# Linear attention into a token-mixing feed-forward layer: U_high x and U_low x as rows of one operand, q's tail at full height, shorter norm statistics, subtractions on VectorE

## The chip, the cores and the metric

The kernel runs on one core of a Trainium2 chip. A core has TensorE (PE: matmuls, with a queue of weight loads of its own, PEld), VectorE (DVE), ScalarE (ACT), GpSimd (POOL) and SyncE (SP, which here issues all DMAs). They run side by side, each through its own instructions in order, and wait for each other by semaphores. The metric is device time in microseconds (us), the median of several runs.

## The reference

Eight batches of 576 tokens. Per batch, 8 heads of linear attention with an RMS norm, and then a layer that mixes tokens through a rank of 32 and applies a feed-forward block:

```python
kv = np.einsum('bhsd,bhse->bhde', k, v)              # 64 x 64 per head
out = np.einsum('bhsd,bhde->bhse', q, kv)            # 576 x 64 per head
rms = np.sqrt(np.mean(out * out, axis=-1, keepdims=True) + 1e-06)
x = (out / rms * g_norm)                             # heads side by side: (8, 576, 512)
h = x.transpose(0, 2, 1) @ U @ V                     # U: 576 x 32, V: 32 x 576
u = x + h.transpose(0, 2, 1)
ch = np.maximum(u @ w_ch1, 0.0) @ w_ch2              # 512 -> 2048 -> 512
return u + ch
```

U, V and the two matrices of the feed-forward block come as float64, everything else as float32.

## The kernel before

**Precision by parts.** TensorE multiplies float32 operands either in float32 or, faster, in a rounded form (`F32R`). For the second, an operand is split into a rounded high part and the low part that is left (`split`, `move` and `minus`), and a product is the sum of high x high, high x low and low x high. Weights arrive as float64 bit patterns and are decoded to float32 by a chain of bit operations (`decode`, five steps, four or five of them on VectorE), then split.

**Attention, per batch b and pair of heads p.** `kv_step` forms k^T v of two heads in one 128x128 block. `out_step` multiplies q by it: q lies transposed (128 rows of two heads, 576 token columns); the first 512 tokens are four float32 matmuls with 128 columns of q as weights (L235, into `big`), the last 64 tokens one with 64 columns (L237, into `small`). The profile records a float32 matmul of the program as two. ScalarE squares both. `stats_step` sums the squares on VectorE, takes the root on ScalarE and sharpens its reciprocal by one Newton step (seven steps on VectorE in all). `mul_step` writes x. `xsplit_step` splits x: `xh` on ScalarE (L102), `xl` for the first 512 tokens on GpSimd (L114), and the low part of the last 64 on VectorE (L278), put in the free lower half of the fifth block of `xh`. `turn_step` transposes x (VectorE and DMAs from batch 1 on, TensorE for batch 0). `t_step` multiplies by U: the weights are a U block of 64 columns, `u2` = [U_high, U_low], so that for batch 1 on the rows 0 to 31 of the result `tp` are U_high x and the rows 32 to 63 U_low x. For batch 0 other weights are used, `u4` = [U_high, U_high] and [U_low, U_low], in 14 matmuls instead of nine. `t4_step` makes of it a 128-row operand of high, high, low and low parts of the sum (for batch 1 on in six steps that go between ScalarE and VectorE), which `mix_step` multiplies by `v4`, V's parts in four matching blocks of rows, and adds to x; the result is scaled by g and split (`split_cols`).

**Feed-forward block.** Tokens go through in nine blocks j of 512. For each of 16 column blocks f of w_ch1, `ffn1` does 12 matmuls of 512 columns (L383 high x high, L384 high x low, L385 low x high); `relu` makes `hh` on ScalarE (L392) and `hl` on VectorE (L393); `ffn2` does 12 more (L400) one f later, when `hl` is there. `finish` adds u on VectorE (L411) and GpSimd (L412) and writes out.

**Order.** Attention of batch b+1 runs between the f of block b (`prep_schedule`). Batch 0 comes ahead of all by a table of positions (`PLAN`), and through block 0 the weights of each f are decoded and split two f ahead (L81 to L95; the low part on GpSimd). `ENG` names the engine of a step by a letter (a, v, g) for each pair. The order that this code gives is rearranged by the framework's own scheduler, with a modelled timeline; the program that comes out is fixed, engine by engine.

Of the kernel before, what the change touches and what calls it, by code (L numbers as in the profile page):

```python
# [47 lines left out]
def build(ctx: ExitStack, tc: tile.TileContext, kv_in, kvt0_in, kvt_in, q_in, uv_in, g_in, w_in, out):  # L48
# [180 lines left out]
    def out_step(b, p):  # L229
# [4 lines left out]
        for i in range(4):  # L234
            nc.tensor.matmul(big[:, i * P:(i + 1) * P], lhsT=qt[:, i * P:(i + 1) * P], rhs=kb, start=True, stop=True)  # L235
# [1 line left out]
        nc.tensor.matmul(small[0:TAIL, 0:P], lhsT=qt[:, MAIN:S], rhs=kb, start=True, stop=True)  # L237
# [4 lines left out]
    def stats_step(b, p):  # L242
        NS = 2 * NT
        ms = sm.tile([P, NS], F32, name="ms")
# [3 lines left out]
        nc.vector.tensor_reduce(out=ms.rearrange("p (i h) -> p i h", h=2), in_=xv, axis=AX.X, op=ALU.add)  # L248
# [3 lines left out]
        nc.vector.tensor_tensor(out=ta, in0=r0, in1=r0, op=ALU.mult)
        nc.vector.tensor_tensor(out=ta, in0=ta, in1=ms, op=ALU.mult)
# [42 lines left out]
    def t_step(b, p):  # L296
        xh, xl = state[b, p]["hl"]
        tp = bank()
        if b == 0:
            todo = [(u, xh, i) for u in u4 for i in range(NT)] + [(u4[0], xl, i) for i in range(4)]  # L300
            for n, (u, xx, i) in enumerate(todo):
                nc.tensor.matmul(tp[0:2 * R, 0:P], lhsT=u[:, i, :], rhs=xx[:, i, :], start=(n == 0), stop=(n == len(todo) - 1))
        else:
            for i in range(NT):
                nc.tensor.matmul(tp[0:2 * R, 0:P], lhsT=u2[:, i, :], rhs=xh[:, i, :], start=(i == 0), stop=(i == NT - 1))  # L305
                if i < 4:
                    nc.tensor.matmul(tp[0:2 * R, 0:P], lhsT=u2[:, i, :], rhs=xl[:, i, :], start=False, stop=False)
# [140 lines left out]
    u4t = weight_slot("u4", [P, 2, NT, 2 * R], F32R, 13)  # L448
    u4 = [u4t[:, n] for n in range(2)]
    for t in u4:  # L450
        nc.gpsimd.memset(t[:, 0, 0:1].bitcast(F32), 0.0)
# [181 lines left out]
```

## Time and profile before

| | |
|---|---|
| Median of three runs | 954.52 us (952.16 to 954.83) |
| Span of the profiled execution, first to last instruction | 949.2 us |
| Time of the profiled execution itself | not listed beside its span; the span is 5.3 us under the median of the runs |
| Mean granted clock of TensorE | 0.993 |
| Busy: PE, PEld, DVE, ACT, POOL | 923.2, 762.1, 439.6, 252.3, 135.4 us |
| Bytes moved by DMA | 65.49 MB |

Busy times are sums over the span; matmuls are pipelined, so their durations overlap and PE's busy time isn't PE at its peak. The start of one matmul to the start of the next is what it takes of TensorE. In rows by stage, a stretch is followed by its length, the busy time and the number of instructions of each engine, and at the end the granted clock, the DMA engines' share and GB/s. In rows of the timeline stand start, duration, engine, line, instruction, and in brackets the idle time ahead with what ended it. Groups of a line show the count, then the total busy us and the mean ns of one, then idle time and what ended it.

### The profile page before, as it was taken

How to read it: one execution, taken by the hardware profiler on the slowest of the kernel's cores; microseconds unless marked ns; L12 is line 12 of the kernel's file. 1: busy time of each engine (PE TensorE's matmuls, PEld its weight loads, DVE VectorE, ACT ScalarE, POOL GpSimd, SP SyncE). 2: the span in 40 equal slices, each digit the busy share in tenths (PEclk: the TensorE clock that was granted, in tenths of full speed). 3: DMA queues.
4: the chain of work that ended last, by engine and by line, in shares of the span. 5: the costliest groups of instructions: out<-in, count | busy, mean ns of one | idle time of the engine just before them, and what ended most of it. 6: DMA issues, size and time to landing. Idle time of an engine off the chain costs nothing.

```text
span 949.2 us, 12251 instructions
## 1 busy us (share of the span) xinstructions
PE 923.2 (97%) x4570; PEld 762.1 (80%) x4570; DVE 439.6 (46%) x881; ACT 252.3 (27%) x535; POOL 135.4 (14%) x119
## 2 busy tenths in 40 slices
PE   8789889999999999999999999999999999999998
PEld 7667678888888888888888888888888888888887
DVE  5999995545354445443454344442543331112112
ACT  5454443322222223222232223222322221111110
POOL 4443430200020002000120002000200020002000
PEclk9999899999999999999999999999999999999999
DMA  9951112312121113221222112211211010001001
GB/s 336 407 203 54 39 46 63 97 54 66 42 95 54 54 35 102 61 59 26 73 72 79 26 54 92 66 41 40 92 50 29 14 45 1 1 0 45 1 1 45
DMA packets 45036, 65.49 MB, mean 69 GB/s; under 512 B 9904, under 2 KB 28080, under 8 KB 44976
## 3 DMA queue, kind: packets, MB, share of 16 engines
q1 hardware_dynamic: 44976, 64.71, 20.9%
q8 instruction: 36, 0.59, 0.3%
q14 instruction: 24, 0.20, 0.1%
HBM read 46.97 MB, written 9.44 MB: 59 GB/s over the span
## 4 chain that ended last, share of the span: by engine, by line
PE 86%; DVE 11%; issue 1%; DMA 1%; ACT 0%; SPq 0%; DVEq 0%; ACTq 0%
PE y L400 38%; PE h L383 13%; PE h L384 13%; PE h L385 13%; DVE dec L87 3%; PE pp L235 2%; PE pp L214 2%; DVE dec L89 2%; DVE dec L85 1%; DVE dec L84 1%; PE pp L237 1%; DMA kvq<-kv_in 1%; PE pp L305 1%; PE pp L375 1%; DVE hl L393 1%
## 5 line engine op out<-in xcount | busy, mean ns | idle before, releaser
L400 PE MATMUL y<-hh,ws 128*128 128x512 f32 (+1 forms) x1072 | 349.6, 393 | 1.7 <-ACT hh L392 1.7
L393 DVE SCALAR_TENSOR_TENSOR hl<-h,hh 128x512 fp32r<-128x512 f32 x142 | 97.9, 690 | 345.3 <-ACT hh L392 344.8
L400 PEld LDWEIGHTS y<-hh,ws 128*128 128x128 f32 x1072 | 194.7, 188 | 39.4 <-ACT hh L392 1.9
L383 PE MATMUL h<-uth,ws 128*128 128x512 f32 x536 | 212.3, 396 | 8.5 <-DVE hl L393 8.5
L385 PE MATMUL h<-uth,ws 128*128 128x512 f32 x536 | 210.6, 393 | 0.5 <-POOL ws L95 0.5
L384 PE MATMUL h<-utl,ws 128*128 128x512 f32 x536 | 210.9, 394 | 0.0
L400 PE MATMUL y<-hl,ws 128*128 128x512 f32 (+1 forms) x536 | 208.3, 389 | 0.0
L392 ACT ACTIVATE hh<-h 128x512 fp32r<-128x512 f32 x142 | 84.8, 597 | 414.8 <-PE h L385 414.7
L383 PEld LDWEIGHTS h<-uth,ws 128*128 128x128 f32 x536 | 101.4, 189 | 32.7 <-DVE hl L393 11.0
L385 PEld LDWEIGHTS h<-uth,ws 128*128 128x128 f32 x536 | 101.6, 190 | 23.1 <-POOL ws L95 0.9
L400 PEld LDWEIGHTS y<-hl,ws 128*128 128x128 f32 x536 | 100.9, 188 | 22.2 <-issue 1.5
L384 PEld LDWEIGHTS h<-utl,ws 128*128 128x128 f32 x536 | 101.5, 189 | 20.6
L114 POOL TENSOR_TENSOR xl<-x,xh 128x512 fp32r<-128x512 f32 x30 | 40.4, 1345 | 499.9 <-ACT xh L102 494.5
L412 POOL TENSOR_TENSOR st<-st,utl 128x512 f32<-128x512 f32 x32 | 41.0, 1302 | 157.9 <-DVE st L411 157.6
L95 POOL TENSOR_TENSOR ws<-dec,ws 128x1024 fp32r<-128x1024 f32 x15 | 37.9, 2527 | 52.2 <-ACT ws L94 46.1
L377 DVE TENSOR_TENSOR ut<-pp,ut 128x288 f32<-128x288 f32 x56 | 24.6, 457 | 30.1 <-DMA ut<-xt 16.9
L411 DVE TENSOR_TENSOR st<-y,uth 128x512 f32<-128x512 f32 x32 | 21.2, 685 | 35.8 <-PE y L400 26.8
L340 ACT ACTIVATE uth<-ut,g_sb 128x448 fp32r<-128x448 f32 (+7 forms) x56 | 27.8, 531 | 37.6 <-DVE ut L377 33.7
L248 DVE TENSOR_REDUCE ms<-x 128x10 f32<-128x640 f32 x32 | 26.0, 813 | 18.0 <-ACT x L239 18.0
L341 DVE SCALAR_TENSOR_TENSOR utl<-ut,g_sb,uth 128x448 fp32r<-128x448 f32 (+7 forms) x56 | 27.3, 514 | 10.1 <-ACT uth L340 7.9
L214 PE MATMUL pp<-kv_sb 128*128 128x128 f32 x232 | 31.4, 275 | 0.0
L102 ACT CAST xh<-x 128x640 fp32r<-128x640 f32 x30 | 21.7, 724 | 33.8 <-DVE x L264 33.8
(202 smaller groups left out, 837.2 us busy)
## 6 DMA issues: line engine op xcount, KB each, us to landing
raw<-w_in SPq DMA_DIRECT2D x30, 512.0 KB, 10.2
kv_sb<-kv_in SPq DMA_DIRECT2D x29, 512.0 KB, 3.5
...
ut<-xt SPq DMA_DIRECT2D x224, 20.0 KB, 1.8
ut<-xt SPq DMA_DIRECT2D x224, 16.0 KB, 1.8
...
```

What stands on the lines that cost most here:

```text
L87: nc.vector.scalar_tensor_tensor(out=bits, in0=high, scalar=0xC0000000, in1=bits, op0=ALU.bitwise_and, op1=ALU.bitwise_or)
L95: lo_eng.tensor_tensor(out=lo, in0=src, in1=hi.bitcast(F32), op=ALU.subtract)
L114: eng.tensor_tensor(out=out, in0=in0, in1=in1, op=ALU.subtract)
L214: nc.tensor.matmul(pp[:, 0:P], lhsT=m[:, i * P:(i + 1) * P], rhs=m[:, MAIN + i * P:MAIN + (i + 1) * P], start=(i == 0 and b < NATIVE), sto ...
L340: nc.scalar.mul(out=hi, in_=src, mul=g_sb)
L383: nc.tensor.matmul(h, lhsT=w1s[f][0][:, d, :], rhs=uh[:, d, :], start=(d == 0), stop=False)
L384: nc.tensor.matmul(h, lhsT=w1s[f][0][:, d, :], rhs=ul[:, d, :], start=False, stop=False)
L385: nc.tensor.matmul(h, lhsT=w1s[f][1][:, d, :], rhs=uh[:, d, :], start=False, stop=(d == ND - 1))
L392: nc.scalar.activation(out=hh, in_=h, func=AF.Relu)
L393: nc.vector.scalar_tensor_tensor(out=hl, in0=h, scalar=0.0, in1=hh.bitcast(F32), op0=ALU.max, op1=ALU.subtract)
L400: nc.tensor.matmul(acc, lhsT=w2s[f][w][:, c, :], rhs=h[:, cols], start=(f == 0 and w == 0 and h is hh), stop=(f == NF - 1 and w == 1))
L412: nc.gpsimd.tensor_tensor(out=o, in0=o, in1=ul[:, c, :].bitcast(F32), op=ALU.add)
```

## The change

It has these parts:

- **q's tail at full height.** The host puts the last 64 tokens of q first. The tail's matmul (now L242) takes the first 128 columns of q as weights, the last 64 tokens and the first 64 of the others; the rows 64 to 127 of its result are not read. The four others follow from column 64.
- **U_high x and U_low x as rows of one operand.** `u4` goes; `u2` is made at once from U and used for batch 0 too, nine matmuls in all pairs, all of `xh` ahead of all of `xl`. `t4_step` no longer sums: its rows are high parts of U_high x and of U_low x (one move), the low part of U_high x (VectorE) and U_high x's high part again (ScalarE). `v4` has V's high part in three blocks of rows and the low part in the fourth, to match.
- **Four-step norm statistics.** The root takes scale and bias on ScalarE; behind the sum and the reciprocal three steps are left on VectorE. The result is too large by -2 x 64, which g makes good: `load_g` scales it once on ScalarE.
- **Subtractions on VectorE.** `xl`, the low parts of w1 and w2 of f = 0, and that of U move there from GpSimd (`ENG`).

```diff
-ENG = dict(kv='aaaaa', xh='aaaaa', xl='ggggg', t4='avva', te='aaaa', uh='vaaa', v4='aggg', wh='avg', wl='ggg', ab='vav', u='agva')
+ENG = dict(kv='aaaaa', xh='aaaaa', xl='vvvvv', t4='avva', te='aaaa', uh='vaaa', v4='aggg', wh='avg', wl='vvv', ab='vav', u='av')
...
+    def load_g():
+        nc.sync.dma_start(out=g_sb, in_=g_in)
+        nc.scalar.mul(out=g_sb, in_=g_sb, mul=-1.0 / (2 * D))
...
-            nc.tensor.matmul(big[:, i * P:(i + 1) * P], lhsT=qt[:, i * P:(i + 1) * P], rhs=kb, start=True, stop=True)
+            nc.tensor.matmul(big[:, i * P:(i + 1) * P], lhsT=qt[:, TAIL + i * P:TAIL + (i + 1) * P], rhs=kb, start=True, stop=True)
         small = bank()
-        nc.tensor.matmul(small[0:TAIL, 0:P], lhsT=qt[:, MAIN:S], rhs=kb, start=True, stop=True)
+        nc.tensor.matmul(small[:, 0:P], lhsT=qt[:, 0:P], rhs=kb, start=True, stop=True)
...
-        nc.vector.tensor_scalar(out=ms, in0=ms, scalar1=1.0 / D, scalar2=1e-6, op0=ALU.mult, op1=ALU.add)
-        nc.scalar.sqrt(out=ta, in_=ms)
+        nc.scalar.activation(out=ta, in_=ss, func=AF.Sqrt, scale=1.0 / D, bias=eps)
         nc.vector.reciprocal(out=r0, in_=ta)
         nc.vector.tensor_tensor(out=ta, in0=r0, in1=r0, op=ALU.mult)
-        nc.vector.tensor_tensor(out=ta, in0=ta, in1=ms, op=ALU.mult)
-        nc.vector.tensor_scalar(out=ta, in0=ta, scalar1=-0.5, scalar2=1.5, op0=ALU.mult, op1=ALU.add)
-        nc.vector.tensor_tensor(out=r0, in0=r0, in1=ta, op=ALU.mult)
+        nc.vector.scalar_tensor_tensor(out=ta, in0=ss, scalar=D * 1e-6, in1=ta, op0=ALU.add, op1=ALU.mult)
+        nc.vector.scalar_tensor_tensor(out=r0, in0=ta, scalar=-3.0 * D, in1=r0, op0=ALU.add, op1=ALU.mult)
...
+        todo = [(xh, i) for i in range(NT)] + [(xl, i) for i in range(4)]
+        for n, (xx, i) in enumerate(todo):
+            nc.tensor.matmul(tp[0:2 * R, 0:P], lhsT=u2[:, i, :], rhs=xx[:, i, :], start=(n == 0), stop=(n == len(todo) - 1))
...
-            ts = sc.tile([R, P], F32, name="ts")
-            nc.scalar.copy(out=ts, in_=tp[R:2 * R, 0:P])
-            nc.vector.tensor_tensor(out=ts, in0=tp[0:R, 0:P], in1=ts, op=ALU.add)
-            nc.scalar.copy(out=t4[0:R], in_=ts)
-            nc.scalar.copy(out=t4[R:2 * R], in_=ts)
-            nc.vector.tensor_tensor(out=t4[2 * R:3 * R], in0=ts, in1=t4[0:R].bitcast(F32), op=ALU.subtract)
-            nc.scalar.copy(out=t4[3 * R:], in_=t4[2 * R:3 * R].bitcast(F32))
+        move("t4", p if b == 0 else -1, t4[0:2 * R], tp[0:2 * R, 0:P])
+        nc.scalar.copy(out=t4[3 * R:], in_=tp[0:R, 0:P])
+        nc.vector.tensor_tensor(out=t4[2 * R:3 * R], in0=tp[0:R, 0:P], in1=t4[0:R].bitcast(F32), op=ALU.subtract)
...
-        move("u", 0, h4, uv4)
-        minus("u", 1, l4, uv4, h4.bitcast(F32))
+        move("u", 0, u2[:, :, 0:R], uvv)
+        minus("u", 1, u2[:, :, R:], uvv, u2[:, :, 0:R].bitcast(F32))
...
-                move("v4", n, v4[n * R:(n + 1) * R, k * VQ:(k + 1) * VQ], vs[k * R:(k + 1) * R, n % 2].bitcast(F32))
+                move("v4", n, v4[n * R:(n + 1) * R, k * VQ:(k + 1) * VQ], vs[k * R:(k + 1) * R, n // 3].bitcast(F32))
...
-        "q_in": qq.transpose(0, 1, 2, 4, 3).reshape(B, NPAIR, P, S),
+        "q_in": np.concatenate([qq[:, :, :, MAIN:], qq[:, :, :, :MAIN]], axis=3).transpose(0, 1, 2, 4, 3).reshape(B, NPAIR, P, S),
```

The scheduler gives a slightly other order. In the rows below a line is followed by the instruction, output<-inputs and the shape of the output; the new program's lines are shifted (L383, L384, L385 and L400 are L372, L373, L374 and L389).

TensorE, the tail's matmul of a pair in the steady part, between two groups of the feed-forward block, before:

```order
L384 MATMUL h<-utl,ws_1166 128x512
L385 MATMUL h<-uth,ws_1166 128x512
L237 MATMUL pp<-kvb_98,q_sb 64x128
L400 MATMUL y<-hl,ws_1102 128x512
L400 MATMUL y<-hh,ws_1102 128x512
```

and of the changed program:

```order
L373 MATMUL h<-utl,ws_1116 128x512
L374 MATMUL h<-uth,ws_1116 128x512
L242 MATMUL pp<-kvb_99,q_sb 128x128
L389 MATMUL y<-hl,ws_1056 128x512
L389 MATMUL y<-hh,ws_1056 128x512
```

It stands in the same place; the output has 128 rows where it had 64.

VectorE, the third pair of batch 4, around the subtraction of x (L262 and L264 write x, L290 transposes it, L278 is the tail's low part, L393 `hl`), before:

```order
L262 TENSOR_TENSOR x<-pp,r_3616 128x512
L264 TENSOR_TENSOR x<-pp,r_3616 64x128
L290 STREAM_TRANSPOSE xt<-x 128x5x4x32
L393 SCALAR_TENSOR_TENSOR hl<-h,hh 128x512
L278 TENSOR_TENSOR xh<-x,xh 64x128
```

and of the changed program (L115 is the subtraction that was GpSimd's, L382 `hl`):

```order
L265 TENSOR_TENSOR x<-pp,r_3506 128x512
L267 TENSOR_TENSOR x<-pp,r_3506 64x128
L293 STREAM_TRANSPOSE xt<-x 128x5x4x32
L115 TENSOR_TENSOR xl<-x,xh 128x512
L281 TENSOR_TENSOR xh<-x,xh 64x128
L382 SCALAR_TENSOR_TENSOR hl<-h,hh 128x512
```

`hl` is now queued behind the subtraction and the tail's low part, which wait for `xh` from ScalarE.

VectorE at the end of the decoding, around the twelfth `hl`, before:

```order
L87 SCALAR_TENSOR_TENSOR dec<-raw_210,dec 128x1024
L290 STREAM_TRANSPOSE xt<-x 128x5x4x32
L278 TENSOR_TENSOR xh<-x,xh 64x128
L89 SCALAR_TENSOR_TENSOR dec<-raw_210,dec 128x1024
L210 TENSOR_TENSOR tails<-kvt_sb,tails 64x128
L211 TENSOR_TENSOR tails<-kvt_sb,tails 128x128
L393 SCALAR_TENSOR_TENSOR hl<-h,hh 128x512
```

and of the changed program (L88 and L90 are the decode's L87 and L89, L366 the addition of `mix_step`):

```order
L366 TENSOR_TENSOR ut_0_89<-pp,ut_0_89 128x288
L86 TENSOR_SCALAR dec<-dec 128x1024
L88 SCALAR_TENSOR_TENSOR dec<-raw_210,dec 128x1024
L382 SCALAR_TENSOR_TENSOR hl<-h,hh 128x512
L90 SCALAR_TENSOR_TENSOR dec<-raw_210,dec 128x1024
```

The twelfth `hl` is ahead of the last decode step, and the two steps on k's and v's tails have gone behind it.

More of the change, by code (lines that the diff above doesn't have):

```diff
@@ L68, in build @@
     v4 = const.tile([P, S], F32R, name="v4")
+    eps = const.tile([P, 1], F32, name="eps")
     kvb = [const.tile([P, P], F32, name=f"kvb{i}") for i in range(2)]
@@ L243, in stats_step @@
         NS = 2 * NT
-        ms = sm.tile([P, NS], F32, name="ms")
+        ss = sm.tile([P, NS], F32, name="ss")
         r0 = sm.tile([P, NS], F32, name="r0")
@@ L247, in stats_step @@
         xv = state[b, p]["x"].rearrange("p i (h e) -> p i h e", e=D)
-        nc.vector.tensor_reduce(out=ms.rearrange("p (i h) -> p i h", h=2), in_=xv, axis=AX.X, op=ALU.add)
-        nc.vector.tensor_scalar(out=ms, in0=ms, scalar1=1.0 / D, scalar2=1e-6, op0=ALU.mult, op1=ALU.add)
-        nc.scalar.sqrt(out=ta, in_=ms)
+        nc.vector.tensor_reduce(out=ss.rearrange("p (i h) -> p i h", h=2), in_=xv, axis=AX.X, op=ALU.add)
+        nc.scalar.activation(out=ta, in_=ss, func=AF.Sqrt, scale=1.0 / D, bias=eps)
         nc.vector.reciprocal(out=r0, in_=ta)
         nc.vector.tensor_tensor(out=ta, in0=r0, in1=r0, op=ALU.mult)
-        nc.vector.tensor_tensor(out=ta, in0=ta, in1=ms, op=ALU.mult)
-        nc.vector.tensor_scalar(out=ta, in0=ta, scalar1=-0.5, scalar2=1.5, op0=ALU.mult, op1=ALU.add)
-        nc.vector.tensor_tensor(out=r0, in0=r0, in1=ta, op=ALU.mult)
+        nc.vector.scalar_tensor_tensor(out=ta, in0=ss, scalar=D * 1e-6, in1=ta, op0=ALU.add, op1=ALU.mult)
+        nc.vector.scalar_tensor_tensor(out=r0, in0=ta, scalar=-3.0 * D, in1=r0, op0=ALU.add, op1=ALU.mult)
         state[b, p]["r"] = r0.rearrange("p (i h) -> p i h", h=2)
@@ L298, in t_step @@
         tp = bank()
[L299 to L307, printed above, removed]
+        todo = [(xh, i) for i in range(NT)] + [(xl, i) for i in range(4)]
+        for n, (xx, i) in enumerate(todo):
+            nc.tensor.matmul(tp[0:2 * R, 0:P], lhsT=u2[:, i, :], rhs=xx[:, i, :], start=(n == 0), stop=(n == len(todo) - 1))
         state[b, p]["tp"] = tp
@@ L427, in build @@
     nc.vector.memset(kvb[0], 0.0)
+    nc.vector.memset(eps, 1e-6)
     spare = ps_h.tile([P, BLK], F32, name="h")
@@ L447, in build @@
         nc.gpsimd.memset(t[:, 0, 0:1].bitcast(F32), 0.0)
[L448 to L451, printed above, removed]
     uvs = weight_slot("uvs", [P, DM], I64, 12)
@@ L457, in build @@
         "uv": lambda: nc.sync.dma_start(out=uvraw, in_=uv_in),
-        "g": lambda: nc.sync.dma_start(out=g_sb, in_=g_in),
+        "g": load_g,
         "kv4": lambda: load_kv(1, 0),
@@ L477, in uv_step @@
         uvv = uv[:, 0:NT * R].rearrange("p (i r) -> p i r", r=R)
-        uv4 = uvv.unsqueeze(2).broadcast_to([P, NT, 2, R])
-        h4, l4 = [u.rearrange("p i (n r) -> p i n r", n=2) for u in u4]
-        move("u", 0, h4, uv4)
-        minus("u", 1, l4, uv4, h4.bitcast(F32))
+        move("u", 0, u2[:, :, 0:R], uvv)
+        minus("u", 1, u2[:, :, R:], uvv, u2[:, :, 0:R].bitcast(F32))
         split(vs[:, 0], vs[:, 1], uv[:, NT * R:], nc.vector)
-    def u2_step():
-        for n in range(2):
-            move("u", 2 + n, u2[:, :, n * R:(n + 1) * R], u4[n][:, :, 0:R].bitcast(F32))
     def v4_step():
@@ L490, in v4_step @@
             for k in range(4):
-                move("v4", n, v4[n * R:(n + 1) * R, k * VQ:(k + 1) * VQ], vs[k * R:(k + 1) * R, n % 2].bitcast(F32))
-    tasks = [(PLAN["uv"], uv_step), (PLAN["v4"], v4_step), (PLAN["u2"], u2_step)]
+                move("v4", n, v4[n * R:(n + 1) * R, k * VQ:(k + 1) * VQ], vs[k * R:(k + 1) * R, n // 3].bitcast(F32))
+    tasks = [(PLAN["uv"], uv_step), (PLAN["v4"], v4_step)]
     for p in range(NPAIR):
```

4 lines of the change are left out of this document (removed).

## The prediction

> **What bounds the kernel now.** I read the page's busy shares first, then the sums by stage, then TensorE's waits, and last the timeline around single matmuls. Busy us, share of the span and instructions of each engine:
>
> ```profile
> PE 923.2 (97%) x4570; PEld 762.1 (80%) x4570; DVE 439.6 (46%) x881; ACT 252.3 (27%) x535; POOL 135.4 (14%) x119
> ```
>
> TensorE (PE) seems to bound everything, but the average hides two stages. The stretch, its length, the busy us of PE, its weight loads (PEld), VectorE (DVE), ScalarE (ACT) and GpSimd (POOL), the granted clock, and DMA:
>
> ```profile
> 50.00:100.00 50.00, 44.22 (x194) 35.04 (x194) 49.59 (x52) 22.54 (x33) 18.99 (x8) 0.93 0.28 101
> 100.00:140.00 40.00, 33.36 (x150) 26.30 (x150) 39.74 (x53) 19.15 (x32) 18.07 (x8) 0.91 0.16 48
> 140.00:200.00 60.00, 60.00 (x307) 49.64 (x307) 35.15 (x82) 18.75 (x45) 8.62 (x8) 1.00 0.27 81
> 200.00:900.00 700.00, 700.00 (x3430) 579.07 (x3429) 268.12 (x606) 161.72 (x363) 66.00 (x51) 1.00 0.16 48
> ```
>
> To 140 us VectorE is busy in 89.33 of 90 us and TensorE is not; from there TensorE has no free time and VectorE has plenty. What TensorE waits for most (total, times, longest), and its last wait:
>
> ```profile
> PE h L383 <- DVE hl L393: 8.5, 5, 2.7
> 138.08 0.50 PE L383 MATMUL h<-uth,ws 128*128 128x512 f32 x1 [1.24 <-DVE hl L393]
> ```
>
> So the end is the place of that last wait (VectorE's work up to 138 us) plus TensorE's own issue pace behind it, where a saved VectorE microsecond is worth nothing.
>
> **The narrow tail matmul (TensorE, behind 138 us).** Start, duration, instruction, in the steady stage:
>
> ```profile
> 433.70 0.39 PE L384 MATMUL h<-utl,ws 128*128 128x512 f32 x1
> 433.93 0.39 PE L385 MATMUL h<-uth,ws 128*128 128x512 f32 x1
> 434.25 0.43 PE L237 MATMUL pp<-kvb,q_sb 128*64 128x128 f32 x2
> 434.61 0.50 PE L400 MATMUL y<-hl,ws 128*128 128x512 f32 x1
> 434.95 0.39 PE L400 MATMUL y<-hh,ws 128*128 128x512 f32 x1
> ```
>
> Durations overlap, so starts are what counts: wide matmuls of 512 columns start 0.23 us apart (433.70 to 433.93). From L385 at 433.93 to the second L400 at 434.95 are 1.02 us, where two wide ones alone take 0.46. So the pair of L237 (the program's one fp32 matmul is recorded as two) costs 0.56 us of TensorE's time, 0.28 for each 128 columns of moving data. The other four matmuls of the same step, which have the same moving operand and 128 columns of weights:
>
> ```profile
> 404.33 1.05 PE L235 MATMUL pp<-kvb,q_sb 128*128 128x128 f32 x8
> 405.14 1.17 PE L400 MATMUL y<-hh,ws 128*128 128x512 f32 x4
> 406.14 0.39 PE L383 MATMUL h<-uth,ws 128*128 128x512 f32 x1
> ```
>
> From the first L235 to the L383 behind the four L400 are 1.81 us; less four wide ones (0.92) that leaves 0.89 for eight, 0.11 each. The new tail has just this form (128 columns of `qt` as weights, fp32, the same `kb`), wherever the order puts it: 0.22 us a pair, a saving of 0.34. How many of these lie behind 138 us (the columns as in the stages above, this line alone):
>
> ```profile
> 138.00:950.00 812.00, 10.81 (x50) 1.00 0.16 49
> ```
>
> 50 records are 25 pairs: 25 x 0.34 = **8.5 us saved**. Bounds: the pair can't become cheaper than its streaming at the wide form's pace, so no more than this; nothing, if the stall isn't due to the width (a rival).
>
> **U x on TensorE.** The nine L305/L307 matmuls stay nine, now high parts first. Their end:
>
> ```profile
> 423.77 0.22 PE L305 MATMUL pp<-xh,u 128*64 128x128 f32 x1
> 423.83 1.14 PE L400 MATMUL y<-hh,ws 128*128 128x512 f32 x4
> 424.80 0.39 PE L383 MATMUL h<-uth,ws 128*128 128x512 f32 x1
> ```
>
> Four wide ones take 0.97 there, 0.05 over 0.92: each piece of the group costs 0.05 beyond its matmuls. In the new order the 24 groups from batch 2 on stand in 44 pieces where there were 39: 5 x 0.05, some **0.3 us lost**. The five matmuls fewer per pair of batch 0 lie before 138 us, beside VectorE: nothing; nor do the six steps of `t4_step` that become three give TensorE anything, since it waits for none of them behind 138 us.
>
> **VectorE before 138 us.** The subtraction for `xl` leaves GpSimd (seven times before 138 us: four pairs of batch 0, three of batch 1), and so do those of w1 and w2: nine of 512 elements. Prices (busy us, mean ns behind the bar):
>
> ```profile
> L411 DVE TENSOR_TENSOR st<-y,uth 128x512 f32<-128x512 f32 x32 | 21.2, 685 | 35.8 <-PE y L400 26.8 <-DMA out<-st 7.1 <-PE pp L385 1.8
> L341 DVE SCALAR_TENSOR_TENSOR utl<-ut,g_sb,uth 128x512 fp32r<-128x512 f32 x4 | 2.7, 746 | 0.6 <-ACT uth L340 0.6
> L253 DVE TENSOR_TENSOR ta<-ta,ms 128x10 f32<-128x10 f32 x32 | 5.7, 178 | 0.9
> ```
>
> Back to back the next starts about 0.08 us before an end, in dependent chains 0.03 behind it, so each occupies 0.61 to 0.78 us; I take 0.65, near L411, the like operation: 5.9 us added (5.5 to 7.0). Removed: two steps of 10 elements in seven statistics, 14 x 0.17 = 2.4 us (1.3 back to back, 2.8 in a chain), and two L320 of 128 elements, some 0.4 (L210 below, of the same length, takes 0.29). The split of u (now 160 elements on VectorE) against the copy of 160 that goes: even. Further removed is what the subtractions on GpSimd did to VectorE:
>
> ```profile
> 18.24 1.37 POOL L114 TENSOR_TENSOR xl<-x,xh 128x512 fp32r<-128x512 f32 x1 [0.43 <-ACT xh L102]
> 18.76 0.87 DVE L252 TENSOR_TENSOR ta<-r 128x10 f32<-128x10 f32 x1
> 22.20 1.34 DVE L278 TENSOR_TENSOR xhl<-x,xhl 64x128 fp32r<-64x128 f32 x1
> ```
>
> A step of 10 elements (0.18 as L253) takes 0.87 while GpSimd subtracts, and one of 128 (0.29 as L210) takes 1.34: 0.7 and 1.05 us lost. If a third of the nine meet VectorE so, 3 us come back (nothing, if another GpSimd operation catches VectorE instead; 3.5 is the most that I find likely). Net 5.9 - 2.4 - 0.4 - 3.0 = +0.1 us; the ends are 5.5 - 2.8 - 0.4 - 3.5 = -1.2 and 7.0 - 1.3 - 0.4 = +5.3. Then the place of the last wait. VectorE ahead of it:
>
> ```profile
> 135.58 1.22 DVE L89 SCALAR_TENSOR_TENSOR dec<-raw,dec 128x1024 uint32<-128x1024 uint32 x1
> 136.83 0.29 DVE L210 TENSOR_TENSOR tails<-kvt_sb,tails 64x128 fp32r<-64x128 f32 x1
> 137.34 0.68 DVE L393 SCALAR_TENSOR_TENSOR hl<-h,hh 128x512 fp32r<-128x512 f32 x1
> ```
>
> In the new order the twelfth `hl` stands ahead of the last L89 (now L90) and the two tail steps, behind one L366 more: 137.34 - 135.58 = 1.76 less 0.45, 1.3 earlier. I take 1.0, since that decode must still be done. The stage gives **-0.9 us** (-2.5 to +5).
>
> **The scaling of g on ScalarE** is a new wait: `xh` of pair 0 is queued behind it. The DMA of g is issued at 6.3 us and lands 8.5 later, at 14.8, before ScalarE gets there:
>
> ```profile
> g_sb<-g_in SPq DMA_DIRECT2D x1, 0.5 KB, 8.5
> 17.44 0.72 ACT L102 CAST xh<-x 128x640 fp32r<-128x640 f32 x1
> ```
>
> It costs its own issue, up to 0.2 us, beside VectorE. The DMA queue keeps its order.
>
> **The sum.** -8.5 + 0.3 - 0.9 = -9.1 us against the 949.2 of the profiled span: 940.1. The runs' median, 954.52, lies 5.3 above that span; I carry this over: **945.4 us**. A difference under 0.3% (2.9 us) can't be told from none here.
>
> **Rivals.** (1) The subtractions cost VectorE their full price and the collisions go on with the weights' splits, which stay on GpSimd:
>
> ```profile
> 74.91 2.40 POOL L95 TENSOR_TENSOR ws<-dec,ws 128x1024 fp32r<-128x1024 f32 x1 [4.41 <-DMA ut<-xt]
> 75.12 3.27 DVE L87 SCALAR_TENSOR_TENSOR dec<-raw,dec 128x1024 uint32<-128x1024 uint32 x1
> ```
>
> A step of the size of L89 (1.22) takes 3.27 here, so each of the 15 splits, one for each f from 1 on, costs some 2 us whichever such step VectorE runs. Then +5 in place of -0.9: 951.3. (2) The reverse: more of those splits meet steps that don't stall:
>
> ```profile
> 53.97 2.37 POOL L95 TENSOR_TENSOR ws<-dec,ws 128x1024 fp32r<-128x1024 f32 x1 [4.76 <-ACT ws L94]
> 54.48 0.81 DVE L248 TENSOR_REDUCE ms<-x 128x10 f32<-128x640 f32 x1
> 55.21 2.22 DVE L87 SCALAR_TENSOR_TENSOR dec<-raw,dec 128x1024 uint32<-128x1024 uint32 x1
> ```
>
> L248 runs through such a split in its usual 0.81, and the L87 behind it loses 1.0 instead of 2.0. Four such meetings more are 4 us less: 941.4. (3) The change doesn't do what it should: the narrow stall isn't due to the width, or the wider load costs in its place:
>
> ```profile
> L235 PEld LDWEIGHTS pp<-kvb,q_sb 128*128 128x128 f32 x224 | 28.4, 191 | 0.8
> L237 PEld LDWEIGHTS pp<-kvb,q_sb 128*64 128x64 f32 x56 | 5.3, 134 | 7.9 <-issue 3.4 <-DVE hl L393 3.2 <-DVE ut L377 0.4
> ```
>
> If loads set the pace, 50 of them grow by 0.057: 954.5 + 2.9 + 0.3 - 0.9 = 956.8. Against it stand the spacings above and the 7.9 us of idle that the narrow loads have and the wide ones don't. The Trainium skill (TensorE: Matmul & The Clock Gate, section LDWEIGHTS) says a load's time grows with its columns alone, by that 53 ns to 107; taken alone it speaks against this change, by some 2.7 us as an estimate from that page. The trace agrees on the loads' direction, not that they decide: wide loads let matmuls start every 0.11 us, and a pair of narrow ones costs 0.56. (4) Slower: `xl` now stands in VectorE's queue ahead of `hl`, which TensorE needs:
>
> ```profile
> 416.80 0.69 DVE L393 SCALAR_TENSOR_TENSOR hl<-h,hh 128x512 fp32r<-128x512 f32 x1
> 417.53 1.43 DVE L278 TENSOR_TENSOR xh<-x,xh 64x128 fp32r<-64x128 f32 x1
> 421.54 0.39 PE L400 MATMUL y<-hl,ws 128*128 128x512 f32 x1
> ```
>
> `hl` ends at 417.49 and is read at 421.54, 4 us of cover. Behind `xl` and the tail step (0.69 + 0.28, after the cast of `xh`) it ends near 419. If the cover were gone, 24 pairs would wait 0.97 us: 945.4 + 23 = 968.7; it decides from 0.38 us a pair.
>
> **How the numbers follow.** Forecast, 943 to 948.5: 0.60. Rival 1, 948.5 to 951.6: 0.14. Rival 2, under 943: 0.15. Rival 3 (956.8): 0.04. Smaller losses together, such as rival 1 with some of rival 4, within 0.3% of before (951.7 to 957.4): 0.04. Rival 4: 0.03. Faster 0.60 + 0.14 + 0.15 = 0.89, same 0.04 + 0.04 = 0.08, slower 0.03. The range takes in rivals 1 and 2 at their worked-out times: 941 to 951.
>
> **What would show it.** The tail's matmuls spaced at 0.11 us with no idle load ahead, and 0.68 us in place of 1.02 from the wide one before to the second behind; TensorE's last wait between 135 and 140 us; no wait of TensorE from 200 to 900. The forecast is wrong if a pair still costs over 0.4 us, if that last wait lies past 143 us, or if new waits on `hl` or `xl` appear behind it.

## The result, and the profile after

Four runs of the changed kernel took 940.8 to 942.5 us, median **941.57**, against 954.26 for the kernel before in runs beside them: a ratio of **0.9881** (95% interval 0.9862 to 0.9901). Forecast was 945.4, range 941 to 951. In every run that lists both, the time is some 1.8 us over the span (1.7 to 1.9); the profiled execution has a span of 939.4 (forecast 940.1) and took 941.2.

The page's busy shares after:

```profile
PE 913.4 (97%) x4550; PEld 763.3 (81%) x4550; DVE 428.2 (46%) x824; ACT 237.6 (25%) x483; POOL 88.7 (9%) x82
```

GpSimd has lost 47 us of work and VectorE, which took some of it over, has 11 us less as well. The same stages as before:

```profile
50.00:100.00 50.00, 44.03 (x203) 34.95 (x202) 49.55 (x51) 23.36 (x32) 17.55 (x7) 0.97 0.28 99
100.00:140.00 40.00, 35.15 (x169) 27.85 (x168) 38.25 (x47) 17.74 (x29) 15.12 (x6) 0.96 0.17 48
140.00:200.00 60.00, 60.00 (x312) 50.61 (x311) 33.23 (x78) 16.95 (x39) 5.17 (x4) 1.00 0.27 83
200.00:900.00 700.00, 699.22 (x3452) 585.06 (x3451) 260.48 (x561) 148.91 (x315) 35.57 (x28) 1.00 0.16 48
```

Still two stages: VectorE has no free time ahead of some 135 us, TensorE none behind. TensorE does 169 matmuls from 100 to 140 where it did 150, and 0.78 us of idle time are new behind 200. Its waits for `hl` (total, times, longest):

```profile
PE h L372 <- DVE hl L382: 6.9, 6, 2.4
```

The last one of the startup, in the timeline:

```profile
134.58 0.50 PE L372 MATMUL h<-uth,ws 128*128 128x512 f32 x1 [0.64 <-DVE hl L382]
```

That wait was at 138.08: **3.5 us** came from the startup. Behind it stand the same 3,969 matmul records in both kernels; they took 811.1 us and now take 804.8: **6.3 us** from TensorE's pace. The tail's matmul in the steady stage:

```profile
417.33 0.39 PE L389 MATMUL y<-hl,ws 128*128 128x512 f32 x1
417.56 0.39 PE L389 MATMUL y<-hh,ws 128*128 128x512 f32 x1
417.79 0.38 PE L242 MATMUL pp<-kvb,q_sb 128*128 128x128 f32 x2
417.93 0.95 PE L389 MATMUL y<-hh,ws 128*128 128x512 f32 x3
```

The pair starts 0.23 us behind the wide matmul ahead of it, as a wide one would; the next wide one starts 0.14 us behind the pair. Before, these were 0.32 and 0.36.

### The profile page after: what moved, and what is told of

Its sections match the earlier page's. It is cut to its first block, busy times and chain, and to the rows that moved or that the text cites. A ratio compares the mean times of both kernels' runs of the same rounds, so it can differ in the third digit from the quotient of the medians.

```text
span 939.4 us, 11992 instructions
## 1 busy us (share of the span) xinstructions
PE 913.4 (97%) x4550; PEld 763.3 (81%) x4550; DVE 428.2 (46%) x824; ACT 237.6 (25%) x483; POOL 88.7 (9%) x82
## 4 chain that ended last, share of the span: by engine, by line
PE 84%; DVE 13%; DMA 1%; issue 1%; SPq 0%; ACT 0%; POOL 0%; DVEq 0%; POOLq 0%
PE y L389 37%; PE h L372 13%; PE h L373 13%; PE h L374 13%; DVE dec L88 3%; PE pp L219 2%; PE pp L240 2%; DVE dec L90 2%; DVE dec L86 2%; PE pp L304 2%; DVE dec L85 1%; DVE hl L382 1%; DMA w1raw<-w_in 1%; PE pp L364 1%; PE pp L389 1%
## 5 line engine op out<-in xcount | busy, mean ns | idle before, releaser
L389 PE MATMUL y<-hh,ws 128*128 128x512 f32 (+1 forms) x1072 | 351.0, 394 | 0.1
L382 DVE SCALAR_TENSOR_TENSOR hl<-h,hh 128x512 fp32r<-128x512 f32 x142 | 97.8, 689 | 307.8 <-ACT hh L381 307.2
L389 PEld LDWEIGHTS y<-hh,ws 128*128 128x128 f32 x1072 | 194.3, 188 | 36.0 <-ACT hh L381 0.8
L372 PE MATMUL h<-uth,ws 128*128 128x512 f32 x536 | 212.5, 397 | 6.9 <-DVE hl L382 6.9
L373 PE MATMUL h<-utl,ws 128*128 128x512 f32 x536 | 210.1, 392 | 0.0
L374 PE MATMUL h<-uth,ws 128*128 128x512 f32 x536 | 209.9, 392 | 0.0
L389 PE MATMUL y<-hl,ws 128*128 128x512 f32 (+1 forms) x536 | 207.6, 387 | 0.0
L372 PEld LDWEIGHTS h<-uth,ws 128*128 128x128 f32 x536 | 101.4, 189 | 31.0 <-DVE hl L382 10.8
L374 PEld LDWEIGHTS h<-uth,ws 128*128 128x128 f32 x536 | 101.2, 189 | 21.9
L373 PEld LDWEIGHTS h<-utl,ws 128*128 128x128 f32 x536 | 101.4, 189 | 20.4
L389 PEld LDWEIGHTS y<-hl,ws 128*128 128x128 f32 x536 | 100.6, 188 | 20.5
L366 DVE TENSOR_TENSOR ut<-pp,ut 128x288 f32<-128x288 f32 x56 | 25.0, 456 | 53.6 <-DMA ut<-xt 39.0
L400 DVE TENSOR_TENSOR st<-y,uth 128x512 f32<-128x512 f32 x32 | 21.2, 686 | 44.5 <-PE y L389 33.0
L330 DVE SCALAR_TENSOR_TENSOR utl<-ut,g_sb,uth 128x448 fp32r<-128x448 f32 (+7 forms) x56 | 28.2, 534 | 14.7 <-ACT uth L329 10.9
L253 DVE TENSOR_REDUCE ss<-x 128x10 f32<-128x640 f32 x32 | 26.1, 814 | 19.0 <-ACT x L244 19.0
L219 PEld LDWEIGHTS pp<-kv_sb 128*128 128x128 f32 x232 | 29.3, 191 | 2.0 <-DVE t L313 0.9
L240 PE MATMUL pp<-kvb,q_sb 128*128 128x128 f32 x224 | 29.6, 274 | 0.0
## 6 DMA issues: line engine op xcount, KB each, us to landing
raw<-w_in SPq DMA_DIRECT2D x30, 512.0 KB, 10.2
```

Source lines behind the costliest of these rows:

```text
L219: nc.tensor.matmul(pp[:, 0:P], lhsT=m[:, i * P:(i + 1) * P], rhs=m[:, MAIN + i * P:MAIN + (i + 1) * P], start=(i == 0 and b < NATIVE), sto ...
L240: nc.tensor.matmul(big[:, i * P:(i + 1) * P], lhsT=qt[:, TAIL + i * P:TAIL + (i + 1) * P], rhs=kb, start=True, stop=True)
L330: nc.vector.scalar_tensor_tensor(out=lo, in0=src, scalar=g_sb, in1=hi.bitcast(F32), op0=ALU.mult, op1=ALU.subtract)
L372: nc.tensor.matmul(h, lhsT=w1s[f][0][:, d, :], rhs=uh[:, d, :], start=(d == 0), stop=False)
L373: nc.tensor.matmul(h, lhsT=w1s[f][0][:, d, :], rhs=ul[:, d, :], start=False, stop=False)
L374: nc.tensor.matmul(h, lhsT=w1s[f][1][:, d, :], rhs=uh[:, d, :], start=False, stop=(d == ND - 1))
```

## How the kernels are compared

The scheduler makes a new order for each version, so a fixed time on the axis is no fair boundary. I priced every matmul by its steady spacing (0.227 us for 512 columns, 0.111 for 128 in float32, 0.060 for a piece of U x, the narrow tail as if it were wide) and noted when 780 us of such work were left. What lies ahead of that is the startup; what the rest takes over 780 us is loss behind it. All from the profiled execution; half-clock time is the time from 25 to 55 us in which the trace shows TensorE at half its clock; "stalls" is how much longer VectorE's steps took than steps of the same shape at their shortest (the tenth percentile), up to its last decode step.

| kernel | ratio (95%) | half clock 25-55 | VectorE stalls | 780 left at | rest |
|---|---|---|---|---|---|
| before | 1 | 1.8 | 32.5 | 151.2 | 798.0 |
| changed | 0.9881 (0.9862-0.9901) | 6.8 | 28.2 | 147.4 | 792.0 |
| E1 tail only | 0.9894 (0.9876-0.9913) | 4.4 | 33.8 | 151.5 | 789.8 |
| E2 subtractions only | 1.0088 (1.0066-1.0109) | 17.1 | 26.8 | 158.3 | 800.3 |
| E3 statistics only | 1.0047 (1.0030-1.0065) | 10.2 | 32.2 | 154.5 | 800.5 |
| E4 U x only | 1.0008 (0.9994-1.0021) | 3.4 | 31.6 | 156.7 | 797.8 |
| E5 changed, splits on VectorE | 0.9810 (0.9789-0.9830) | 6.8 | 2.8 | 134.3 | 797.5 |
| E6 changed, subtractions back | 0.9940 (0.9921-0.9958) | 10.2 | 29.5 | 149.6 | 793.3 |
| E7 changed, old statistics | 1.0053 (1.0034-1.0071) | 18.8 | 26.9 | 160.8 | 792.9 |
| E8 changed, 96-column tail | 0.9898 (0.9882-0.9915) | 6.8 | 27.3 | 147.9 | 792.0 |
| E9 subtractions and statistics | 1.0043 (1.0026-1.0060) | 10.2 | 28.8 | 158.9 | 800.1 |
| E10 before, splits on VectorE | 0.9805 (0.9789-0.9820) | 3.4 | 6.4 | 132.0 | 801.7 |
| E11 E5 with two `kv_sb` | 0.9736 (0.9716-0.9756) | 6.8 | 2.9 | 136.3 | 792.0 |
| E12 E10 with two `kv_sb` and the tail | 0.9744 (0.9726-0.9761) | 6.8 | 7.0 | 134.0 | 794.6 |

The runs of before beside them had medians of 951.6 to 954.3 us at different times, so kernels are compared by their ratios. The column from 25 to 55 us leaves out half clock that falls elsewhere: up to 200 us it is 13.7 us before and in the changed kernel, 23.9 in E2, 20.5 in E3, 27.3 in E4, E7 and E9, 10.2 in E5 and 3.4 in E10.

## Experiments: the parts one by one

**E1, the tail alone.** Lines L235 and L237 and the order of q's columns:

```diff
-        nc.tensor.matmul(small[0:TAIL, 0:P], lhsT=qt[:, MAIN:S], rhs=kb, start=True, stop=True)
+        nc.tensor.matmul(small[:, 0:P], lhsT=qt[:, 0:P], rhs=kb, start=True, stop=True)
```

> The kernel before, with the tail of q at full height (128 columns of weights instead of 64) and nothing else changed. Theory (a narrow fp32 matmul costs TensorE its stall wherever it stands): the 25 pairs behind the last startup wait give back 0.33 us each by the starts in the two traces, 8.2 us; VectorE does the same work, so the last startup wait stays at 138.1 us (within 0.5). About 946.1 us against 954.3. Rival A (the stall went because of the other parts, such as the new order of U x): no gain, 954 us, and the pairs still cost over 0.4 us. Rival B (the whole 12.7 us come from here, since the 20 narrow ones ahead of the last wait held VectorE up as well): 941 to 942 us and a last wait near 134.6.

Measured 943.14 us beside 954.19. TensorE around the tail, and its last wait of the startup:

```profile
430.47 0.39 PE L385 MATMUL h<-uth,ws 128*128 128x512 f32 x1
430.70 0.38 PE L237 MATMUL pp<-kvb,q_sb 128*128 128x128 f32 x2
430.84 0.48 PE L400 MATMUL y<-hl,ws 128*128 128x512 f32 x1
431.15 0.40 PE L400 MATMUL y<-hh,ws 128*128 128x512 f32 x1
138.67 0.50 PE L383 MATMUL h<-uth,ws 128*128 128x512 f32 x1 [1.26 <-DVE hl L393]
```

From L385 to the second L400 are 0.68 us, which were 1.02. The rest is 8.2 us shorter, to the tenth what the theory said; the startup isn't (138.67, 0.6 later), so rival B falls, and A too. The runs' ratio says 10.1 us (8.3 to 11.8), 2 more than the trace; the profiled execution of before lies at the low end of its runs (below), so that the difference of the two spans (7.9) is the smaller.

**E8, what in the narrow tail stalls.** The changed kernel with `lhsT=qt[:, 0:96]` and `small[0:96]`:

> The changed kernel, with 96 columns of q as the tail's weights instead of 128 (the extra columns aren't used by either; 64 columns cost 0.33 us more a pair). Theory (a float32 matmul with less than 128 columns of weights makes TensorE finish what is in it before its load): the stall is there in full, entry 0.31 to 0.32 us, 0.16 between the two, 0.20 behind, so 8 us more than the changed kernel, 949.5 us. Rival A (the cost goes with the columns that are missing): half of it, 4 us, 945.5 us. Rival B (only 64 or fewer columns stall, since they take another tiling of the array): 941.6 us, with 0.23, 0.11 and 0.03 us as at 128 columns. Loads alone: 96 columns load faster than 128, no more than 1 us gained.

Rival B came true. The tail in this kernel:

```profile
417.93 0.39 PE L389 MATMUL y<-hh,ws 128*128 128x512 f32 x1
418.16 0.38 PE L242 MATMUL pp<-kvb,q_sb 128*96 128x128 f32 x2
418.29 0.94 PE L389 MATMUL y<-hh,ws 128*128 128x512 f32 x3
```

Its weight loads from 200 to 900 us, as a group (shape, count, busy us, mean ns, idle ahead):

```profile
L242 PEld LDWEIGHTS pp<-kvb,q_sb 128*96 128x96 f32 x44 | 6.9, 162 | 1.8
```

The same group in the kernel before:

```profile
L237 PEld LDWEIGHTS pp<-kvb,q_sb 128*64 128x64 f32 x44 | 4.2, 134 | 6.6 <-DVE hl L393 3.2 <-issue 2.5 <-DVE ut L377 0.4
```

At 96 columns the pair enters in 0.23 us and leaves in 0.13, as at 128, and the rest takes 792.0 us in both kernels. So neither the missing columns nor the length of the load costs anything (162 ns against 189 at 128 columns makes no difference): only 64 columns stall, with 6.6 us of idle ahead of the loads against 1.8. The Trainium skill (TensorEngine Tiling (Array Packing), Key Properties and When to Use Tiling) says that weights of 64 columns or fewer can take another tiling mode and that a change of mode drains TensorE. The 64 and 96 agree with it; U x doesn't, whose weights have 64 columns too, in the rounded form, and which enters in 0.23 us and leaves within 0.06 in the kernel before. What sets float32 apart there wasn't tried.

**E4, U x as rows of one operand, alone.** `t_step`, `t4_step`, `u2` and `v4` as in the change:

> The kernel before, with only U_high x and U_low x as rows of one operand (five matmuls fewer per pair of batch 0, high parts first, three steps instead of six behind them). The prediction's terms: 0.3 us lost on TensorE behind the last wait and 0.4 gained on VectorE ahead of it: 954.2 us. Theory after the result: the pieces of U x cost 0.9 us behind the last wait instead of 0.3, so 954.8 us, and if the new order at a block's end (four subtractions for utl ahead of hl on VectorE) comes with this part, two waits on hl near 574 and 675 us and 0.8 us more, 955.6. Rival (the missing 2.6 us of the startup come from here, since VectorE and ScalarE lose steps ahead of the last wait): 951.7 us.

954.69 beside 954.19: nothing measurable. The rest is 0.2 us shorter, not longer; this order has one piece of U x more and not five. The startup of the profiled execution is 5.5 us longer, but that is one with TensorE at half clock from 10.8 to 21.0 us; the twelve runs lie from 951.6 to 956.3.

**E2 and E3, the subtractions and the statistics alone.**

```diff
-ENG = dict(... xl='ggggg', ... wl='ggg', ...)
+ENG = dict(... xl='vvvvv', ... wl='vvv', ...)
```

> The kernel before, with only the subtractions for xl and for the first weights w1 and w2 on VectorE instead of GpSimd. The prediction's term: VectorE is given 5.9 us before 138 us and gets 3.0 back from collisions, so the last startup wait moves to about 141 and the time to 957.2 us. Theory after the result (VectorE's lost time before the last wait fell by 4.5 us, nearly all in the 10-element steps that met GpSimd's subtractions): +1 to +2 us, 955.3 to 956.3. Rival (this part alone gives the 3.5 us by which the startup came out shorter): 950.8 us, last wait at 134.6.

> The kernel before, with only the four-step norm statistics (and g scaled on ScalarE). The prediction's term: two steps of 10 elements fewer in each of seven statistics before 138 us, 2.4 us, last wait near 135.7 and 951.9 us; the steady part unchanged. Rival A (the statistics still meet GpSimd's subtractions, which stay, so that the shorter chain is eaten by the next step's stall): within 0.7 us of 954.3. Rival B (a removed step is one that had stalled, so each is worth more than 0.17 us): 950 us or less.

Both expectations failed: each alone makes the kernel *slower*, E2 by 0.88% and E3 by 0.47%. VectorE's stalls fell in E2 as foreseen (32.5 to 26.8 us). What came up is a wait of TensorE, and with it the clock. The stretch from 30 to 50 us, columns as above (PE, PEld, DVE, ACT, POOL, granted clock, DMA): of before,

```profile
30.00:50.00 20.00, 17.11 (x107) 13.36 (x105) 18.17 (x26) 10.94 (x22) 11.01 (x9) 1.00 1.03 409
```

of E2,

```profile
30.00:50.00 20.00, 11.08 (x52) 9.27 (x50) 18.85 (x31) 7.51 (x10) 4.66 (x2) 0.61 0.99 392
```

of E3,

```profile
30.00:50.00 20.00, 16.37 (x72) 12.89 (x72) 15.12 (x20) 8.84 (x17) 10.07 (x8) 0.74 1.03 409
```

and of the changed kernel:

```profile
30.00:50.00 20.00, 17.18 (x83) 14.47 (x84) 18.30 (x25) 11.13 (x25) 8.11 (x6) 0.83 1.03 409
```

TensorE does 107 matmuls there before, 52 in E2 and 72 in E3; their kinds differ, so the priced work is the better measure. At 50 us 858.7 us of it are left before, 858.9 in the changed kernel, 860.5 in E3 and 866.0 in E2: E2's whole delay of some 7 us is there by then. VectorE's order made most of it. The first 10-element step of one pair's statistics, the x that follows from them, and TensorE's wait for this x, before,

```profile
26.82 0.17 DVE L249 TENSOR_SCALAR ms<-ms 128x10 f32<-128x10 f32 x1
32.98 0.68 DVE L262 TENSOR_TENSOR x<-y,r 128x512 f32<-128x512 f32 x1
33.81 1.13 PE L287 MATMUL pp<-ident,x 128*128 128x128 f32 x8 [0.30 <-DVE x L262]
```

and in E2:

```profile
28.14 0.16 DVE L249 TENSOR_SCALAR ms<-ms 128x10 f32<-128x10 f32 x1
42.84 0.69 DVE L262 TENSOR_TENSOR x<-y,r 128x512 f32<-128x512 f32 x1
43.67 2.05 PE L287 MATMUL pp<-ident,x 128*128 128x128 f32 x8 [6.23 <-DVE x L262]
```

In E2 the scheduler puts eight decode steps of 1024 elements between the seven steps of these statistics, where before it puts none. TensorE's waits from 30 to 50 us are 8.9 us in E2 and 2.9 before. The half clock comes behind a wait and not ahead of it: it sets in at 35.5 us in E2, inside the wait of 2.7 us for `st` that begins at 33.5, and in the 3.4 us ahead of it TensorE is busy only 43% of the time.

E3 is another case. In spite of its 10.2 us of half clock it is only 0.9 us behind at 100 us and 1.0 at 140. Most of its 3.3 us at the 780 mark come from two waits behind 140 us, 1.6 for `hl` and 0.8 for `xl`. What put them there isn't settled.

The rest costs 2.3 and 2.5 us more in E2 and E3, of which some 1.4 in new waits, by the starts. In E3, of VectorE and of TensorE:

```profile
584.91 2.21 DVE L344 SCALAR_TENSOR_TENSOR utl<-ut,g_sb,uth 128x384 fp32r<-128x384 f32 x4 [1.41 <-POOL st L415]
587.03 0.69 DVE L396 SCALAR_TENSOR_TENSOR hl<-h,hh 128x512 fp32r<-128x512 f32 x1
587.77 0.50 PE L386 MATMUL h<-uth,ws 128*128 128x512 f32 x1 [0.38 <-DVE hl L396]
```

The changed kernel has two of them:

```profile
571.52 2.21 DVE L330 SCALAR_TENSOR_TENSOR utl<-ut,g_sb,uth 128x384 fp32r<-128x384 f32 x4 [1.41 <-POOL st L401]
573.65 0.68 DVE L382 SCALAR_TENSOR_TENSOR hl<-h,hh 128x512 fp32r<-128x512 f32 x1
574.38 0.50 PE L372 MATMUL h<-uth,ws 128*128 128x512 f32 x1 [0.38 <-DVE hl L382]
```

At a block's end the scheduler puts four subtractions for `utl` ahead of `hl`, where before, E1 and E4 have `hl` first. `xl` has no part in it: in E3 it is still GpSimd's.

**E9, E6 and E7: the two together, and each undone in the changed kernel.**

> The kernel before, with the subtractions for xl, w1 and w2 on VectorE and the four-step statistics, but the tail of q and U x as before. Alone the two cost 6.8 and 3.5 us. If they add: 10.3 us slower, a ratio of 1.011. Theory (they don't: with long statistics VectorE's queue is so full from 20 to 50 us that TensorE runs dry and falls to half clock for 14 to 17 us, with short ones and GpSimd's subtractions for 10, with both moved only for 3 to 7): the ratio is 0.995 to 1.003, the first 840 us of remaining matmul work are reached near 78 us instead of 84.5, and no half-clock window from 25 to 55 us is longer than 7 us.

> The changed kernel, with the subtractions for xl and the first w1 and w2 back on GpSimd. Alone, in the kernel before, their move to VectorE cost 6.8 us. Theory 1 (that price holds in the changed kernel too and other parts pay for it): 935 us. Theory 2 (what a part costs in the startup depends on the order that the scheduler makes and on where the half-clock windows fall, so the parts don't add): any sign, within 5 us of 941.6; VectorE's stalls before its stage ends go up by about 5 us and its own work down by about 6. Rival (in the changed kernel the move is what brings the startup forward, as the prediction's collision term has it): 944.5 to 947 us.

> The changed kernel, with the statistics in their old seven steps and g unscaled. Alone, in the kernel before, the four-step form cost 3.5 us. Theory 1 (that holds here as well): 938 us. Theory 2 (order and clock windows; in the changed kernel nothing on GpSimd meets the chain of 10-element steps any more, so two steps fewer are worth their 2.4 us of VectorE): 944 us. Rival (no effect, since the saved steps lie beside other work): 941.6 within 1.5 us.

E9 is 1.0043, between the sum (1.0135 by the measured ratios) and the theory's 0.995 to 1.003: the parts don't add, but the theory was wrong on how far; 840 us were left at 83.9 us and not near 78. The other two say the same from the other side. With old statistics the subtractions on VectorE cost 0.9%; with the new ones nothing (E3 to E9); with the new ones, the tail and U x they *gain* 0.6% (E6 to changed, where the price of E2 would have made E6 faster). The four-step statistics cost 0.5% alone and gain 1.7% in the changed kernel (E7). None of E7's three expectations came near its 957.21 us. E6's 946.08 us is the time that its rival gave (944.5 to 947), but its stalls rose by only 1.3 us, so collisions alone can't be the reason. Both kernels with old statistics and the subtractions on VectorE, E2 and E7, have the wait of 6.2 us for that x, the long half-clock stretch (17.1 and 18.8 us) and their 780 mark 7 to 13 us late; that is the one pattern that repeats. The waits from 30 to 50 us explain most of E2's 7 us and about half of E7's 13. Why U x and the tail, worth nothing in the startup alone, bring the mark from 158.9 (E9) to 147.4 isn't settled: order, half-clock time and stalls all changed at once, and E9's profiled execution, the slowest of its ten, had another 10.2 us of half clock from 10.7.

## Experiments: what VectorE loses to GpSimd

**E5 and E10, the weights' low parts on VectorE**, in the changed kernel and in the kernel before:

```diff
-        split(w[:, 0], w[:, 1], t, nc.gpsimd)
+        split(w[:, 0], w[:, 1], t, nc.vector)
```

> The changed kernel, with the weights' low parts (the subtraction of 1024 elements for each f from 1 on) on VectorE instead of GpSimd. Theory (VectorE's steps that read two operands from SBUF stop while GpSimd subtracts; in the changed kernel VectorE still loses 29.7 us so before 147 us, some 2 us for each split): each split costs VectorE about 1.25 us of its own (an L88 or L90 of the same length takes 1.22) and gives back 2.0, so 14 of them make VectorE's stage some 10 us shorter and the kernel 932 us (930 to 935); no VectorE step of a kind takes over 1.2 times its shortest. Rival A (the long VectorE steps are due to something else, such as DMA or ScalarE): VectorE is given 17 us more before its stage ends, 955 us or more. Rival B (TensorE, or the half-clock windows, bounds the stage as closely as VectorE does): 938 to 941 us although VectorE is freed.

> The kernel before, with only the weights' low parts (1024 elements for each f from 1 on) on VectorE instead of GpSimd. Theory (the splits on GpSimd cost VectorE 2.0 us each, and 1.25 on VectorE itself): VectorE's stalls before its last decode fall from 32.4 us to about 10 (those from the subtractions for xl, w1 and w2 stay), its own work grows by 18, net 4 to 5 us less, and the ratio is 0.990 to 0.996. Rival (the price of a stall is paid by something else that takes its place, and the gain in the changed kernel came from its order): ratio 1.000 or more.

E5 took 933.51 us beside 951.57, the time that was foreseen, but not by the sum foreseen: VectorE's last decode step came 8.0 us earlier where I had 10, the 780 mark 13.1 earlier, and the rest took 5.5 us more. VectorE's groups from 50 to 127 us, of the changed kernel,

```profile
L88 DVE SCALAR_TENSOR_TENSOR dec<-raw,dec 128x1024 uint32<-128x1024 uint32 x11 | 24.0, 2186 | 0.1
L86 DVE TENSOR_SCALAR dec<-dec 128x1024 uint32<-128x1024 uint32 x11 | 13.4, 1220 | 0.2
L253 DVE TENSOR_REDUCE ss<-x 128x10 f32<-128x640 f32 x3 | 2.4, 810 | 0.0
```

and of E5:

```profile
L88 DVE SCALAR_TENSOR_TENSOR dec<-raw,dec 128x1024 uint32<-128x1024 uint32 x12 | 14.6, 1217 | 0.1
L96 DVE TENSOR_TENSOR ws<-dec,ws 128x1024 fp32r<-128x1024 f32 x12 | 14.6, 1216 | 0.3 <-ACT ws L95 0.2
L86 DVE TENSOR_SCALAR dec<-dec 128x1024 uint32<-128x1024 uint32 x11 | 7.5, 683 | 0.1
L253 DVE TENSOR_REDUCE ss<-x 128x10 f32<-128x640 f32 x3 | 2.4, 814 | 0.0
```

The same step takes 2186 ns or 1217, another 1220 or 683, with nothing changed in the program but the engine of the split and the order that the scheduler makes of it; the reduction takes 810 and 814. With 1.22 us for the added step and 2.0 no longer lost, stalls fall from 28.2 to 2.8 us: GpSimd's subtractions caused nearly all of them. The Trainium skill (GPSIMD Engine Reference, 1. Specifications) says that GpSimd shares its SBUF interfaces with VectorE and contends with its two-input steps and with those in a two-port mode; the two-input step that slows down (L88) and the one-input reduction that doesn't agree with it. Whether L86, which has one input and slows down too, runs in such a mode no run here shows.

E10 beats its expectation by far: 0.9805 where I had 0.990 to 0.996. VectorE gave what was priced: stalls fell to 6.4 us and its last decode step came 5.7 us earlier (131.1 for 136.8). The 780 mark came 19 us earlier. The rest is TensorE's: one half-clock window of 3.4 us is left in the whole startup, and from 50 to 100 us it is busy in 49.8 of 50 us. I had not priced that. Two things account for the 19 us: from 50 to 140 us TensorE's waits fall from 12.4 to 0.2 us, and 13.7 us of half clock fall to none, worth up to half of that, 6.8 (an estimate from the half rate). E10 equals E5, though E5 has the tail and E10 hasn't.

**E11 and E12, better versions.** In E5 TensorE lost 5.9 us behind its startup. TensorE's wait (total, times, longest):

```profile
PE pp L219 <- DMA kv_sb<-kv_in: 3.4, 1, 3.4
```

The load's issue on the DMA queue, behind output writes:

```profile
152.64 1.05 SPq L402 DMA_DIRECT2D out<-st  x1
153.78 0.38 SPq L128 DMA_DIRECT2D kv_sb<-kv_in  x1
```

E11 gives `kv_sb` a second buffer (`bufs=2`); E12 is the kernel before with that, the splits on VectorE and the tail at full height.

> The changed kernel with the splits on VectorE, and two buffers instead of one for a pair's k and v (kv_sb). In the run with one buffer TensorE lost 5.9 us near 158 us: 3.4 waiting for a load of kv_sb that the DMA queue issued only at 153.8, behind output writes, and 1.4 ahead of it. Theory: with a second buffer the load is issued one step earlier and the 3 to 5 us come back, ratio to the kernel before 0.976 to 0.978 (with one buffer 0.981). Rival A (the load waits for the queue and not for the buffer, so another buffer changes nothing): 0.981. Rival B (the new order costs elsewhere what it gains here): 0.981 or more, with no wait on kv_sb but new ones on hl.

> The kernel before with three edits: the tail of q at full height, the weights' low parts on VectorE, two buffers for kv_sb; U x, the statistics and the subtractions for xl, w1 and w2 stay as before. Theory (once the splits are off GpSimd, the other parts of the change gain nothing: 0.981 without them and without the tail, 0.981 with all of them): the 8.2 us of the tail add to 0.9805 whatever the startup does, since they lie behind it, and 2 to 4 us come from the buffer, ratio 0.968 to 0.971, about 924 us. Rival A (the parts depend on each other, and subtractions, statistics and U x are needed for a short startup): no better than 0.9736, which all parts with the splits and the buffer gave. Rival B (the second buffer's order costs this startup what it gains): 0.972.

From 140 to 200 us, TensorE in E5 and then in E11:

```profile
140.00:200.00 60.00, 55.12 (x295) 46.30 (x294) 31.68 (x72) 15.88 (x37) 5.09 (x4) 1.00 0.26 80
```

```profile
140.00:200.00 60.00, 60.00 (x315) 50.92 (x314) 32.80 (x75) 15.90 (x37) 5.59 (x4) 1.00 0.28 89
```

E11 is **929.03 us** beside 953.36, the wait gone, and better than the 0.976 to 0.978 expected: the rest is 5.5 us shorter than E5's, the startup 2.0 longer. E12 is 927.78 beside 951.83, the same within the intervals, and not the 0.968 to 0.971 that I expected. Its tail gives what it should (1.7 to 2.0 us lost in each of the three stretches from 760 us left to 200, where E10 loses 4.0 to 4.7). But 5.0 us are still lost right behind the 780 mark, 2.0 of them in a wait for `kvb` that E10 has too, so the buffer took nothing away there; and the startup is 2 us longer, with 13.7 us of half clock in its first 35 us where E10 has 3.4. The time is rival A's, the reason isn't: E12's 780 mark comes 2.3 us ahead of E11's, so the other parts aren't needed for a short startup. Neither version beats the other; both beat the changed kernel by some 1.4%.

## Why the prediction was right, point by point

- **What bounds the kernel**: right, and E5 and E10 show it: 25 and 26 us of stalls taken from VectorE, for some 18 us of added work, moved the 780 mark by 13 and 19 us. VectorE's last decode step itself came 8.0 and 5.7 us earlier; the rest is TensorE's waits and its clock.
- **The narrow tail, -8.5 us**: right. By the starts 8.2 us, the pair from 1.02 to 0.68 us as forecast. Rival 3 is out, load rule included (E8).
- **U x, +0.3 us**: alone it costs nothing (E4). In the changed kernel's order there are 46 pieces against 41, five more as forecast, but they cost 0.5 to 0.9 us, by what is counted with them: 0.4 between the pieces' own matmuls, 0.1 at their entries, the rest not clearly theirs.
- **"No wait of TensorE from 200 to 900"**: wrong. Two waits on `hl`, 0.8 us by the profile and 1.1 by the starts. Rival 4 had this wait, for another reason: not `xl` ahead of `hl` but `utl`. The prediction named new waits on `hl` as a sign that it is wrong; in this point it is. With U x they make the steady gain 6.3 where the forecast had 8.2.
- **VectorE before 138 us, +0.1**: to its last decode step it was -1.1 (136.8 to 135.7): its own work +4.8 us (the forecast had 5.9 - 2.4 - 0.4 = +3.1), stalls -4.3 (the forecast gave 3.0 back), idle -1.1 (steps overlap a little, so these don't add exactly). The mechanism of the stalls is right: the moved subtractions had cost VectorE 4.0 us of them, and these are gone. The scaling of g cost nothing, as forecast: 0.19 us on ScalarE at 15.50, which then waits 0.39 us for x.
- **The place of `hl`, -1.0**: -2.4. It ended 1.2 us behind the last decode step and now ends 1.2 ahead of it. Together -3.5 instead of -0.9; the last wait at 134.58 lies just under the 135 to 140 given.
- **Why that was near enough**: two errors, -2.6 in the startup and +1.9 behind it, nearly cancel, so the span came out at 939.4 for 940.1. And the method, a sum of prices for parts, isn't borne out in the startup: E2, E3 and E7 show that the same part is a loss or a gain by what stands beside it. The prediction could not see that from one profile of one order; it was right there by luck.
- **Rivals 1 and 2**: the measured 941.57 lies outside the forecast's own 943 to 948.5. It is inside the range because rival 2, at 941.4, was taken into it, and rival 2's mechanism isn't what happened: all 14 splits ahead of the last decode step still stall a VectorE step, 26.0 us in all where it was 27.2, not 4 us less. Rival 1 was right that these collisions go on, and wrong on the price.
- **The carried-over 5.3 us from span to median**: the step that made 3.5 of the 3.8 us by which the number is too high. Time less span is some 1.8 us in every run; the other 3.5 were the luck of before's profiled execution, 949.2 + 1.8 = 951.0, where 17 runs beside E1 lie from 950.95 to 955.84. It should have been carried over as 1.8, with the rest as spread.
